# Windowed attention and a MoE layer on one core: V strips as the stationary operand, and all engines ordered by a list scheduler

## The chip, the cores and the metric

The kernel runs on one core of one Trainium2 chip. A core has five engines that run beside each other, each in its own order: TensorE (PE: matmuls into PSUM, eight banks of 128 x 512 float32), VectorE (DVE), ScalarE (ACT), GpSimd (POOL, which here issues the loads that change the type from float32 to float16) and SyncE (SP, which issues the other transfers). A pool or ring of n buffers lets n uses of a tile be under way; the next use waits for the oldest. The metric is the device time of one execution in microseconds (us).

## The reference

There are 8 batches, 8 heads of 64, 512 local and 32 global tokens for each batch. A local query sees the 32 global keys and the local keys at a distance of at most 32; a global query sees all 544 keys. The result goes, as x, through a layer with the hard-swish function:

```python
s_ll = np.where(np.abs(pos[:, None] - pos[None, :]) <= 32, s_ll, -1000000000.0)
s_l = np.concatenate([s_lg, s_ll], axis=-1)            # global keys first
out_l = np.matmul(sm(s_l), np.concatenate([v_g, v_l], axis=2))
out_g = np.matmul(sm(s_g), v_all)                      # 32 queries, 544 keys
x = np.concatenate([out_g, out_l], axis=2)             # as rows of tokens: 4352 x 512
h = x @ w_in                                           # 512 x 2048
out = (h * np.clip(h + 3.0, 0.0, 6.0) / 6.0) @ w_out   # 2048 x 512
```

sm is softmax with the maximum taken off first.

## The kernel before

**Loads.** GpSimd loads q and k of a batch in pieces of 128 tokens (L98), v into a tile ve of five blocks with a column of ones beside each head (L110), then w_in in 4 pieces (L125) and w_out in 16 (L129), all in one queue. After batch 0's loads come the weights; the loads of batch b + 1 are issued three at a time in the loop over blocks of batch b. SyncE copies ve into vo, the same values moved by 64 tokens (L114, L115).

**Attention** goes in blocks. A local block is 128 queries of four heads, as two halves of 64 queries; a half sees 128 local keys and the 32 global ones. There are eight local blocks and two global ones (four heads each) in a batch. For a local block PE makes 16 score matmuls on 64x64 tiles (L202); DVE adds a mask and takes a minimum for each head (L210); ACT takes exp into float16 (L213); DVE packs the global columns of the four heads together (L215); PE turns five 128x128 pieces (L221, L223) into one of two PSUM buffers t; ACT copies them to et (L226); PE multiplies them with the values, global ones first (L231), then eight matmuls of 65 columns with ve and vo as the moving operand (L241); the 65th column is the sum of the weights, by which DVE divides (L255, L256). After two blocks PE turns x (L264) and DVE copies it into xt (L268). q and k are turned at the end of the batch ahead, one pair of heads at a time (L180), and copied by ACT (L183).

**MoE.** For 512 tokens there are 16 first groups of four matmuls (L332), each followed by a relu on ACT (L335) and a product on DVE (L336), and 16 second groups of four matmuls (L346) with a copy (L350) and a store after each four. Groups use three PSUM buffers m. The global tokens of all batches go through it at the end.

**Order.** The loop at L413 to L462 writes each engine's order by hand: for block i it emits the scores of block i, the values of block i - 2, the transposes of block i - 1, and three or four times `fill(0.8)`, which takes MoE groups from a list as shares add up to one. PSUM's eight banks: m 3, s 2, t 2, a 1.

Of the kernel before, what the change touches and what calls it, by code (L numbers as in the profile page):

```python
# [10 lines left out]
FP16 = mybir.dt.float16  # L11


@with_exitstack
def kernel(
# [20 lines left out]
    NQD = NP // 2  # L36
    NJ = Sl // P
    NDFF = dff // P
    HW = 64
    U = Sg + P  # L40
    D1 = D + 2
    KC = Sl + 2 * Sg
# [7 lines left out]
    AX = mybir.AxisListType.XY  # L50

    constp = ctx.enter_context(tc.tile_pool(name="constp", bufs=1))
    natp = ctx.enter_context(tc.tile_pool(name="natp", bufs=2))
    wrk = ctx.enter_context(tc.tile_pool(name="wrk", bufs=2))
    small = ctx.enter_context(tc.tile_pool(name="small", bufs=12))
    xtp = ctx.enter_context(tc.tile_pool(name="xtp", bufs=2))
    moep = ctx.enter_context(tc.tile_pool(name="moep", bufs=1))
    moew = ctx.enter_context(tc.tile_pool(name="moew", bufs=4))
# [6 lines left out]
    qk = [[constp.tile([P, 2 * KC], FP16, tag=f"qk{r}_{p}", name=f"qk{r}_{p}") for p in range(NP)]  # L65
          for r in range(2)]
    ve = [constp.tile([P, NJ + 1, H, D1], FP16, tag=f"ve{r}", name=f"ve{r}") for r in range(2)]
    vo = [constp.tile([P, NJ, H, D1], FP16, tag=f"vo{r}", name=f"vo{r}") for r in range(2)]
    vgb = [constp.tile([P, NQD, 4 * D1], FP16, tag=f"vgb{r}", name=f"vgb{r}") for r in range(2)]
    xg = constp.tile([P, NP, B * Sg], FP16, tag="xg", name="xg")  # L70
    egs = [constp.tile([P, 5 * P], FP16, tag=f"eg{e}", name=f"eg{e}") for e in range(2)]
    ident = constp.tile([P, P], FP16, tag="ident", name="ident")
    masks = [constp.tile([P, U], FP32, tag=f"mask{i}", name=f"mask{i}") for i in range(3)]

    w_in_t = [moep.tile([P, dff], FP16, tag=f"win{m}", name=f"win{m}") for m in range(NP)]
    w_out_t = [moep.tile([P, dm], FP16, tag=f"wout{c}", name=f"wout{c}") for c in range(NDFF)]

    state = {b: {} for b in range(B)}


    def qk_loads(b):
        st = state[b]
        work = []
        if b % 2 == 0:
            t = natp.tile([P, H * D], FP16, tag="qkg", name="qkg")
            for i in range(2):
                for k, src in enumerate((q_g, k_g)):
                    r0 = i * 2 * Sg + k * Sg
                    work.append((t[r0:r0 + Sg, :].rearrange("s (h d) -> s h d", d=D),
                                 src[b + i].rearrange("h s d -> s h d")))  # L90
            st["qkg"] = t
        st["qn"] = natp.tile([P, NJ, H * D], FP16, tag="qn", name="qn")
        st["kn"] = natp.tile([P, NJ, H * D], FP16, tag="kn", name="kn")
        for j in range(NJ):
            for t, src in ((st["qn"], q_l), (st["kn"], k_l)):
                work.append((t[:, j, :].rearrange("s (h d) -> s h d", d=D),
                             src[b, :, j * P:(j + 1) * P, :].rearrange("h s d -> s h d")))
        return [lambda o=o, i=i: nc.gpsimd.dma_start(out=o, in_=i) for o, i in work]  # L98

    def v_loads(b):  # L100
        r = b % 2
        vgn = natp.tile([P, NQD, D], FP16, tag="vgn", name="vgn")
        work = [(vgn, v_g[b].rearrange("(q h) g d -> (h g) q d", q=NQD)),
                (ve[r][0:Sg, 0, :, 0:D], v_g[b].rearrange("h s d -> s h d"))]

        for i in range(NJ + 1):
            p0, p1 = (Sg if i == 0 else 0), (Sg if i == NJ else P)
            s0 = i * P - Sg
            work.append((ve[r][p0:p1, i, :, 0:D], v_l[b, :, s0 + p0:s0 + p1, :].rearrange("h s d -> s h d")))
        work = [lambda o=o, i=i: nc.gpsimd.dma_start(out=o, in_=i) for o, i in work]  # L110

        def shift():

            nc.sync.dma_start(out=vo[r][0:HW, :, :, :], in_=ve[r][HW:P, 0:NJ, :, :])  # L114
            nc.sync.dma_start(out=vo[r][HW:P, :, :, :], in_=ve[r][0:HW, 1:NJ + 1, :, :])  # L115

        def blocks():
            for h in range(4):
                nc.vector.tensor_copy(out=vgb[r][h * Sg:(h + 1) * Sg, :, h * D1:h * D1 + D],  # L119
                                      in_=vgn[h * Sg:(h + 1) * Sg, :, :])  # L120
        return work[0:2] + work[2:] + [shift, blocks]

    def load_w_in():
        for m in range(NP):
            nc.gpsimd.dma_start(out=w_in_t[m], in_=moe_w_in[m * P:(m + 1) * P, :])  # L125

    def load_w_out():
        for c in range(NDFF):
            nc.gpsimd.dma_start(out=w_out_t[c], in_=moe_w_out[c * P:(c + 1) * P, :])  # L129

    def band():

        m = masks[1]
        nc.vector.memset(m, 0.0)
        for s in range(2):
            w = m[s * HW:(s + 1) * HW, Sg:U]
            nc.gpsimd.affine_select(out=w, in_=w, compare_op=ALU.is_ge, fill=OUTSIDE,
                                    base=0, pattern=[[1, P]], channel_multiplier=-1)
            nc.gpsimd.affine_select(out=w, in_=w, compare_op=ALU.is_ge, fill=OUTSIDE,
                                    base=HW, pattern=[[-1, P]], channel_multiplier=1)  # L140
        nc.vector.tensor_copy(out=masks[0], in_=m)
        nc.vector.memset(masks[0][0:HW, Sg:2 * Sg], OUTSIDE)
        nc.vector.tensor_copy(out=masks[2], in_=m)
        nc.vector.memset(masks[2][HW:P, U - Sg:U], OUTSIDE)

    def clear(r):
        nc.vector.memset(ve[r][:, NJ, :, :], 0.0)
        nc.vector.memset(ve[r][:, 0:NJ, :, D:D1], 1.0)
        nc.vector.memset(ve[r][0:Sg, NJ, :, D:D1], 1.0)
        nc.vector.memset(egs[r][:, S:], 0.0)  # L150
        nc.vector.memset(vgb[r], 0.0)
        for h in range(4):
            nc.vector.memset(vgb[r][h * Sg:(h + 1) * Sg, :, h * D1 + D:h * D1 + D + 1], 1.0)
        for p in range(NP):
            for c0 in (KC, 2 * KC - Sg):
                nc.vector.memset(qk[r][p][:, c0:c0 + Sg], 0.0)


    def t_tile(cols):
        t = pst.tile([P, 1024], FP16, tag="t", name="t")  # L160
        return t[:, 0:cols]

    def global_qk(b):
        st = state[b]
        ps = t_tile(NP * P)
        for p in range(NP):
            nc.tensor.matmul(out=ps[:, p * P:(p + 1) * P], lhsT=st["qkg"][:, p * P:(p + 1) * P],
                             rhs=ident, is_transpose=True)
        gt = wrk.tile([P, NP, P], FP16, tag="gt", name="gt")
        nc.scalar.copy(out=gt.rearrange("d p c -> d (p c)"), in_=ps)  # L170
        state[b]["gt"] = gt
        state[b + 1]["gt"] = gt

    def pair_qk(b, p):
        st = state[b]
        ps = t_tile(2 * Sl)
        for i, nat in enumerate((st["qn"], st["kn"])):
            for j in range(NJ):
                c0 = i * Sl + j * P
                nc.tensor.matmul(out=ps[:, c0:c0 + P], lhsT=nat[:, j, p * P:(p + 1) * P],  # L180
                                 rhs=ident, is_transpose=True)
        dst = qk[b % 2][p].rearrange("d (i c) -> d i c", i=2)[:, :, Sg:Sg + Sl]
        nc.scalar.copy(out=dst, in_=ps.rearrange("d (i s) -> d i s", i=2))  # L183

    def local_scores(b, j, qd):
        st = state[b]
        gc = (b % 2) * 2 * Sg + Sg
        ps = pss.tile([P, 2, 512], FP32, tag="s", name="s")
        for pi in range(2):
            p = 2 * qd + pi  # L190
            t = qk[b % 2][p]
            for w, (c0, n) in enumerate(((0, Sg), (Sg, P))):
                for s in range(2):
                    for e in range(2):
                        rows = slice(e * D, (e + 1) * D)
                        lhs = t[rows, Sg + j * P + s * HW:Sg + j * P + (s + 1) * HW]
                        if w == 0:
# [297 lines left out]
```

## Time and profile before

| | |
|---|---|
| median of the runs | 400.8 us (3 runs, 400.43 to 402.07) |
| span of the profiled execution | 400.1 us |
| instructions | 10480 |
| granted TensorE clock, mean | 0.999 |
| GpSimd busy | 120.0 us |
| GB/s of the transfers over the span | 79 |

The span is the profiled execution's own time from its first to its last instruction; 0.7 us lie between it and the median. A row of the busy time by stretches gives the stretch, its length, then for PE, PE's weight loads, DVE, ACT and POOL the busy time and the number of instructions, then the granted clock, the share of the DMA engines and GB/s. A row of the chain or the timeline gives the start in us, the time in us, and the engine, line and operation. A group's row gives busy us, the mean ns of one, and the idle time ahead of them with what ended it.

### The profile page before, as it was taken

What the parts mean: (1) busy time and instruction counts of PE and PEld (TensorE: products, weight loads), DVE (VectorE), ACT (ScalarE), POOL (GpSimd) and SP (SyncE); (2) the same over time, 40 slices, a digit from 0 to 9 for tenths busy, and PEclk for the clock granted to TensorE, in tenths of its full rate; (3) what the DMA queues carried; (4) which work ended last, traced back from release to release, by engine and by line L of the source; (5) the groups of instructions that cost most, each with busy time, mean ns of one, the idle gap of its engine ahead of it and who ended that gap; (6) DMA issues with size and microseconds to landing.
All of it is one profiled execution on the core that took longest, in us unless ns stands there. A gap on an engine that the chain in (4) does not pass through costs nothing.

```text
span 400.1 us, 10480 instructions
## 1 busy us (share of the span) xinstructions
PE 364.8 (91%) x4104; PEld 203.6 (51%) x4104; DVE 263.9 (66%) x1073; ACT 255.0 (64%) x549; POOL 120.0 (30%) x166
## 2 busy tenths in 40 slices
PE   0647499999999999999999999999999999999996
PEld 0414286655455555555555545555555455545642
DVE  2426368866797569766995788658965698457611
ACT  1554389866687569756885588657875687346400
POOL 8924999834700290009200740004000000000000
PEclk9999999999999999999999999999999999999999
DMA  9999999984930199019901992019201000100022
GB/s 91 87 210 189 154 144 162 166 74 63 173 67 28 31 159 111 3 54 129 140 7 54 91 127 56 28 54 90 51 28 55 27 2 28 51 32 0 2 79 79
DMA packets 117874, 31.75 MB, mean 79 GB/s; under 512 B 109888, under 2 KB 111936, under 8 KB 117824
## 3 DMA queue, kind: packets, MB, share of 16 engines
q0 software_dynamic: 111552, 17.84, 60.2%
q1 hardware_dynamic: 6272, 13.24, 10.3%
q8 instruction: 32, 0.52, 0.5%
q14 instruction: 18, 0.15, 0.1%
HBM read 35.65 MB, written 8.91 MB: 111 GB/s over the span
## 4 chain that ended last, share of the span: by engine, by line
PE 75%; ACT 6%; DVE 5%; POOL 5%; DMA 5%; issue 2%; POOLq 0%; ACTq 0%
PE m L346 29%; PE m L332 23%; PE t L221 4%; DMA win<-in_moe_w_in_dram 4%; PE s L202 4%; PE a L241 3%; PE t L180 3%; ACT ex L213 3%; ACT t L335 2%; DVE gt L336 2%; PE a L231 2%; PE t L298 2%; DVE ot L350 1%; DMA qn<-in_q_l_dram 1%; PE t L264 1%
## 5 line engine op out<-in xcount | busy, mean ns | idle before, releaser
L332 PE MATMUL m<-xt,win 128*128 128x512 f16 (+1 forms) x576 | 123.1, 358 | 3.0 <-DVE gt L336 2.1
L346 PE MATMUL m<-wout,gt 128*128 128x512 f16 x512 | 121.8, 379 | 0.0
L213 ACT ACTIVATE ex<-sm,mx 128x160 f16<-128x160 f32 x256 | 89.4, 418 | 43.5 <-DVE mx L210 43.4
L336 DVE SCALAR_TENSOR_TENSOR gt<-t,m 128x512 f16<-128x512 f32 (+1 forms) x144 | 85.7, 623 | 18.9 <-ACT t L335 18.3
L335 ACT ACTIVATE t<-m 128x512 f32<-128x512 f32 (+1 forms) x160 | 79.5, 529 | 25.3 <-PE m L332 23.9
L332 PEld LDWEIGHTS <-win 128*128 128x128 f16 x640 | 60.5, 98 | 49.8 <-issue 4.7
L210 DVE CUSTOM_DVE_ANT_0 sm<-s,mask 128x160 f32<-128x160 f32 x256 | 68.4, 319 | 8.4 <-PE s L202 7.5
L346 PEld LDWEIGHTS <-gt 128*128 128x128 f16 x512 | 47.2, 98 | 44.4
L226 ACT COPY et<-t 128x640 f16<-128x640 f16 x64 | 43.9, 686 | 21.2 <-PE t L223 21.2
L350 DVE COPY ot<-m 128x512 f32<-128x512 f32 x34 | 23.5, 691 | 36.6 <-PE m L346 36.6
L98 POOL DMA_DIRECT2D qn<-in_q_l_dram x32 | 29.7, 928 | 33.3 <-PE t L180 32.3
L183 ACT COPY qk<-t 128x1024 f16<-128x1024 f16 x32 | 31.9, 1008 | 11.0 <-PE t L180 11.0
L221 PE MATMUL t<-ident,ex 128*128 128x128 f16 x256 | 31.1, 229 | 2.4 <-ACT ex L213 1.8
L110 POOL DMA_DIRECT2D ve<-in_v_l_dram x40 | 32.4, 855 | 1.0 <-issue 0.4
L98 POOL DMA_DIRECT2D kn<-in_k_l_dram x32 | 29.8, 930 | 0.0
L202 PEld LDWEIGHTS <-qk 64*64 64x64 f16 x1024 | 17.7, 111 | 23.4 <-issue 14.7
L180 PE MATMUL t<-ident,qn 128*128 128x128 f16 x128 | 14.2, 231 | 15.2 <-POOL ident masks.py:199 9.6
L256 DVE TENSOR_TENSOR x<-a,rec 128x256 f16<-128x256 f32 x64 | 27.0, 421 | 1.1
L241 PE MATMUL a<-vo,et 128*64 128x65 f16 x256 | 20.8, 205 | 6.3 <-DMA vo<-ve 6.3
L110 POOL DMA_DIRECT2D vgn<-in_v_g_dram x8 | 6.0, 749 | 68.5 <-DVE vgb L119 68.5
L202 PE MATMUL s<-qk 64*64 64x128 f16 x512 | 25.6, 230 | 0.0
L215 DVE COPY exg<-ex 128x128 f16<-128x128 f16 x64 | 15.4, 240 | 14.8 <-ACT ex L213 14.1
(68 smaller groups left out, 379.9 us busy)
## 6 DMA issues: line engine op xcount, KB each, us to landing
out_dram<-ot SPq DMA_DIRECT2D x32, 256.0 KB, 2.0
vo<-ve SPq DMA_DIRECT2D x16, 264.0 KB, 3.8
qn<-in_q_l_dram POOLq DMA_DIRECT2D x32, 128.0 KB, 5.3
kn<-in_k_l_dram POOLq DMA_DIRECT2D x32, 128.0 KB, 5.7
ve<-in_v_l_dram POOLq DMA_DIRECT2D x24, 128.0 KB, 5.4
win<-in_moe_w_in_dram POOLq DMA_DIRECT2D x4, 512.0 KB, 13.0
wout<-in_moe_w_out_dram POOLq DMA_DIRECT2D x16, 128.0 KB, 5.0
ve<-in_v_l_dram POOLq DMA_DIRECT2D x8, 96.0 KB, 5.2
```

The costliest lines, as they stand in the source:

```text
L98: return [lambda o=o, i=i: nc.gpsimd.dma_start(out=o, in_=i) for o, i in work]
L110: work = [lambda o=o, i=i: nc.gpsimd.dma_start(out=o, in_=i) for o, i in work]
L202: nc.tensor.matmul(out=ps[s * HW:(s + 1) * HW, e, pi * U + c0:pi * U + c0 + n], lhsT=lhs, rhs=rhs)
L210: nc.vector.tensor_tensor_reduce(out=sm, in0=ps[:, e, pi * U:(pi + 1) * U], in1=m, scale=-scale, scalar=3.0e38, op0=ALU.add, op1=ALU.min, ...
L213: nc.scalar.activation(out=ex[:, h, :], in_=sm, func=EXP, scale=-1.0, bias=mx)
L221: nc.tensor.matmul(out=ps[:, h * P:(h + 1) * P], lhsT=ex[:, h, Sg:U], rhs=ident, is_transpose=True)
L226: nc.scalar.copy(out=et, in_=ps)
L241: nc.tensor.matmul(out=ps[s * HW:(s + 1) * HW, h, 0:D + 1], lhsT=et[:, h * P + s * HW:h * P + (s + 1) * HW], rhs=v[:, j, 4 * qd + h, 0:D + 1],
L332: nc.tensor.matmul(out=ps[:, 0:n], lhsT=w_in_t[m][:, c * P:(c + 1) * P], rhs=x[:, m, 0:n], start=(m == 0), stop=(m == NP - 1))
L335: nc.scalar.activation(out=t1[:, 0:n], in_=ps[:, 0:n], func=RELU, bias=0.5, scale=1.0 / 6.0)
L336: nc.vector.scalar_tensor_tensor(out=g[:, 0:n], in0=t1[:, 0:n], scalar=1.0, in1=ps[:, 0:n], op0=ALU.min, op1=ALU.mult)
L346: nc.tensor.matmul(out=ps, lhsT=gs[c][:, t0:t0 + P], rhs=w_out_t[c], start=(c == 0), stop=(c == NDFF - 1))
```

## The change

The kernel is written anew around the same arithmetic of the MoE part.

- **A unit** is 32 queries of one head with 32 global and 96 local keys: 128 keys. A local step is 128 queries of all eight heads, 32 units. There are four local steps in a batch.
- **Scores**: eight full-array matmuls with 32 columns take the global keys, laid out with zeros for the other head of the pair (kgz), and 32 matmuls on 64x32 tiles with 96 columns take the local keys.
- **Softmax**: the minimum for each head as before but over 128 columns; exp writes float32 in place and also gives the sum; DVE takes reciprocals and scales each head into float16, before the transposes. No column of ones.
- **Transposes**: eight of 128x128 for a step, into the only PSUM buffer T (1024 columns), copied by DVE.
- **Values**: SyncE lays V out as strips st, one of 128 keys for each 32 queries (16 strips of 128 x 512 in float16 for a batch; the 32 global rows are repeated in each). A strip's two heads are the stationary operand and the weights of 64 columns stream: 16 matmuls for a step. The result is x transposed; ACT copies it into xt in two half-partition copies. PE no longer turns x. The global queries use V as the stationary operand too.
- **Loads**: w_in comes in 16 pieces, by quarters of its columns; batch 1's q, k and v are issued ahead of w_out.
- **PSUM**: S 2 banks, T 1, A 2, M 3.
- **Order**: every operation is added to a plan with an engine, a duration, what it needs, a key and the buffers that it takes and gives back. `lay()` runs through the plan once and gives every engine its order; the instructions are emitted in that order.

The core of the diff (helpers for evictions, loads and the global steps are left out where the text above tells them):

```diff
-    psm = ctx.enter_context(tc.tile_pool(name="psm", bufs=3, space=bass.MemoryType.PSUM))
-    pss = ctx.enter_context(tc.tile_pool(name="pss", bufs=1, space=bass.MemoryType.PSUM))
-    pst = ctx.enter_context(tc.tile_pool(name="pst", bufs=2, space=bass.MemoryType.PSUM))
-    psa = ctx.enter_context(tc.tile_pool(name="psa", bufs=1, space=bass.MemoryType.PSUM))
+    psS = many(1, [P, 2, 512], FP32, "s", pp)
+    psT = many(1, [P, 1024], FP16, "t", pp)
+    psA = many(1, [P, 2, 512], FP32, "a", pp)
+    psM = many(3, [P, 512], FP32, "m", pp)
...
+    nat = many(3, [P, 2, HD], FP16, "nat")
...
+    st = many(2, [P, NJ * NU, HD], FP16, "st")
+    sm = many(NS, [P, H, P], FP32, "sm")
+    pn = many(NS, [P, H, P], FP16, "pn")
...
+    LAT = {"PE": 260, "ACT": 170, "DVE": 140, "POOL": 150, "SP": 0, "Q": 0}
...
+    def lay(self):
...
+        while done < len(self.ops):
+            best = None
+            for e, cand in opened.items():
+                if not cand:
+                    continue
+                if e in ("POOL", "SP"):
+                    pool = [min(cand, key=lambda o: (o.key, o.n))]
+                else:
+                    pool = cand
...
+                s0 = min(s for s, _ in starts)
+                s, o = min(((s, o) for s, o in starts if s <= s0 + 40), key=lambda x: (x[1].key, x[1].n))
+                if best is None or s < best[0]:
+                    best = (s, o)
...
+        order.sort(key=lambda o: (o.start, o.n))
+        return order
...
+    def strips(b, js, key):
...
+            if j0 == 0:
+                nc.sync.dma_start(out=st[r][0:G, :, :], in_=ve[r][0:G, 0:1, :].to_broadcast([G, NJ * NU, HD]))
+            v4 = st[r].rearrange("p (j u) c -> p j u c", u=NU)
+            for c in range(NU):
+                lo = c * UQ
+                a = min(P - lo, KL)
+                nc.sync.dma_start(out=v4[G:G + a, j0:j1, c, :], in_=ve[r][lo:lo + a, j0:j1, :])
+                if a < KL:
+                    nc.sync.dma_start(out=v4[G + a:P, j0:j1, c, :], in_=ve[r][0:KL - a, j0 + 1:j1 + 1, :])
...
+    def local_step(b, j, key):
...
+            for p in range(NP):
+                for e in range(2):
+                    nc.tensor.matmul(out=ps[:, e, p * P:p * P + G],
+                                     lhsT=qk[r][:, p, 0, UQ + j * P:UQ + (j + 1) * P], rhs=kgz[r][:, p, e, :])
+            for p in range(NP):
+                for u in range(NU):
+                    for e in range(2):
+                        rows = slice(e * D, (e + 1) * D)
+                        q0 = UQ + j * P + u * UQ
+                        nc.tensor.matmul(out=ps[u * UQ:(u + 1) * UQ, e, p * P + G:(p + 1) * P],
+                                         lhsT=qk[r][rows, p, 0, q0:q0 + UQ],
+                                         rhs=qk[r][rows, p, 1, q0 - UQ:q0 + 2 * UQ])
+        s = add("PE", 800, pe, [qkT[b, j], qkT[b, min(j + 1, NJ - 1)], kg[b]], key=key, acq="S")
...
+                nc.vector.tensor_tensor_reduce(
+                    out=sm[sm_op.slot][:, h, :], in0=psS[s.slot][:, e, p * P:(p + 1) * P], in1=m,
+                    scale=-scale, scalar=3.0e38, op0=ALU.add, op1=ALU.min,
+                    accum_out=stat[stat_op.slot][:, 0, h:h + 1])
...
+                nc.scalar.activation(out=sm[sm_op.slot][:, h, :], in_=sm[sm_op.slot][:, h, :], func=EXP,
+                                     scale=-1.0, bias=stat[stat_op.slot][:, 0, h:h + 1],
+                                     accum_out=stat[stat_op.slot][:, 1, h:h + 1])
...
+                    nc.vector.tensor_scalar(out=pn[pn_op.slot][:, h, :], in0=sm[sm_op.slot][:, h, :],
+                                            scalar1=stat[stat_op.slot][:, 2, h:h + 1], scalar2=None, op0=ALU.mult)
...
+            for h in range(H):
+                nc.tensor.matmul(out=psT[op.slot][:, h * P:(h + 1) * P], lhsT=pn[pn_op.slot][:, h, :],
+                                 rhs=ident, is_transpose=True)
...
+            nc.vector.tensor_copy(out=et[et_op.slot].rearrange("k h q -> k (h q)"), in_=psT[t.slot])
...
+                    nc.tensor.matmul(out=ps[:, p // 2, c0:c0 + 64],
+                                     lhsT=st[r][:, j * NU + u, p * P:(p + 1) * P],
+                                     rhs=et[et_op.slot][:, 2 * p:2 * p + 2, u * UQ:(u + 1) * UQ])
...
+            nc.scalar.copy(out=xt[xt_op[b].slot][e * D:(e + 1) * D, :, j * P:(j + 1) * P].rearrange(
+                "d p (u q) -> d p u q", u=NU), in_=src[e * D:(e + 1) * D, :, :, e, :])
...
+    for b in range(B):
+        base = -8.0 if b == 0 else -5.5 if b == 1 else 4.0 * b - 7.0
...
+                wi[g] = load_w_in(g, -6.0 + 0.1 * g)
...
+                wo[c] = load_w_out(c, -4.0 + 0.05 * c)
...
+        moe_local(b, lead + 4.5, 4.0)
+    moe_global(lead + 6.5, 1.5)
...
+    order = plan.lay()
```

More of the change, by code (lines that the diff above doesn't have):

```diff
@@ L68 @@
[L68 to L85, printed above, removed]
+    AX = mybir.AxisListType.X
+    sb = ctx.enter_context(tc.tile_pool(name="sb", bufs=1))
+    pp = ctx.enter_context(tc.tile_pool(name="pp", bufs=1, space=bass.MemoryType.PSUM))
@@ L98, in qk_loads @@
-        return [lambda o=o, i=i: nc.gpsimd.dma_start(out=o, in_=i) for o, i in work]
-    def v_loads(b):
-        r = b % 2
[L102 to L121, printed above, removed]
@@ L146, in clear @@
[L146 to L156, printed above, removed]
@@ L159, in t_tile @@
[L159 to L172, printed above, removed]
@@ L185, in local_scores @@
[L185 to L193, printed above, removed]
+                    nc.gpsimd.dma_start(out=dst(op, i, k), in_=src[b + i].rearrange("h s d -> s h d"))
+        return add("POOL", 2300, emit, [], key=key, acq="natg", xfer=800)
@@ L339 @@
-    held = {}
-    def second(gs, t0, quarter, store):
-        if quarter == 0:
-            held["ps"] = psm.tile([P, 512], FP32, tag="m", name="m")
-        ps = held["ps"]
-        for c in range(quarter * 4, quarter * 4 + 4):
-            nc.tensor.matmul(out=ps, lhsT=gs[c][:, t0:t0 + P], rhs=w_out_t[c],
-                             start=(c == 0), stop=(c == NDFF - 1))
-        if quarter == 3:
-            ot = moew.tile([P, dm], FP32, tag="ot", name="ot")
-            nc.vector.tensor_copy(out=ot, in_=ps)
-            store(ot)
@@ new lines, in moe_local, with key @@
+    def moe_local(b, at, span):
+        set_ = add("ACT", 0, lambda op: None, xdone[b, 0], key=at - 1, acq="gs")
+        n = 256 if b == 0 else 512
+        total = 16 * (Sl // n) + 16
+        k = [0]
+        def key():
+            k[0] += 1
+            return at + span * k[0] / total
+        done = [[] for _ in range(NDFF)]
+        per = n // P
+        for part in range(Sl // n):
+            xdeps = [d for j in range(part * per, (part + 1) * per) for d in xdone[b, j]]
+            for c in range(NDFF):
+                done[c].append(first(c, n, part * n, lambda: xt[xt_op[b].slot], xdeps,
+                                     [xt_op[b]], set_, key()))
+        for j in range(NJ):
+            row = b * S + G + j * P
+            second(j * P, [done[c][j // per] for c in range(NDFF)], set_,
+                   [(out[row:row + P, :], 0, P)], [key() for _ in range(4)])
@@ L370, in moe_global @@
+    def moe_global(at, span):
+        deps = [xgd[b] for b in range(B)]
+        set_ = add("ACT", 0, lambda op: None, deps, key=at - 1, acq="gs")
+        done = [first(c, B * G, 0, lambda: xg, deps, [], set_, at + span * c / 24) for c in range(NDFF)]
         rows = out.rearrange("(b s) d -> b s d", s=S)
+        per = P // G
         for i in range(B // per):
-            def store(ot, i=i):
-                for b in range(per):
-                    nc.sync.dma_start(out=rows[i * per + b, 0:Sg, :], in_=ot[b * Sg:(b + 1) * Sg, :])
```

684 lines of the change are left out of this document (410 added, 274 removed).

## The prediction

> **What bounds the kernel now.** I read the page's summary first, then the busy time by stretches, the chain that ended last, and the order of TensorE's work in one steady stretch.
>
> ```profile
> span 400.1 us, 10480 instructions
> ...
> PE 364.8 (91%) x4104; PEld 203.6 (51%) x4104; DVE 263.9 (66%) x1073; ACT 255.0 (64%) x549; POOL 120.0 (30%) x166
> ```
> ```profile
> 0.00:20.00 20.00, 6.78 (x73) 4.91 (x73) 6.64 (x57) 7.18 (x11) 18.65 (x34) 1.00 1.39 89
> 20.00:40.00 20.00, 11.76 (x170) 6.77 (x170) 9.29 (x60) 10.74 (x27) 6.83 (x13) 1.00 1.09 200
> 40.00:60.00 20.00, 14.32 (x162) 10.51 (x159) 10.07 (x37) 11.98 (x27) 20.00 (x28) 1.00 1.82 149
> ...
> 200.00:300.00 100.00, 99.28 (x1151) 53.96 (x1149) 74.73 (x304) 73.44 (x157) 16.13 (x20) 1.00 0.46 59
> ```
> ```profile
> 19.37 15.98 DMA win<-in_moe_w_in_dram
> ...
> 41.57 5.41 DMA qn<-in_q_l_dram
> 48.25 1.44 PE m L332 x6
> ...
> 105.66 1.02 PE m L332 x4
> ...
> 316.59 1.02 PE m L332 x4
> ...
> 375.69 20.73 PE m L346 x96
> ```
>
> There are two regimes. In the first 60 us PE is busy for 32.9 us (first column of busy time), and the chain runs through transfers: w_in lands at 35.35 us, and from 41.57 to 46.98 us everything waits for the next batch's q. The first MoE matmul starts at 48.25 us. After that PE is the bound: 99% busy from 200 to 300 us, DVE 75%, ACT 73%. Like places of the batches stand five batches apart at 105.66 and 316.59 us, so a batch takes 42.2 us. A 512-column MoE matmul costs 20.73 / 96 = 0.216 us, and a batch has 64 of each kind: 27.7 us. The other 14.5 us are attention and gaps; the change works on these and on the head.
>
> ```profile
> 208.10 0.39 PE L180 MATMUL t<-ident,qn 128*128 128x128 f16 x4
> ...
> 208.55 1.89 PE L346 MATMUL m<-wout,gt 128*128 128x512 f16 x8
> ...
> 220.03 0.22 PE L283 MATMUL s<-gt 64*32 64x32 f16 x4
> 220.07 0.29 PE L284 MATMUL s<-qk,gt 64*32 64x240 f16 x4
> 220.17 0.30 PE L285 MATMUL s<-qk,gt 64*32 64x272 f16 x4
> 220.41 0.22 PE L241 MATMUL a<-ve,et 128*64 128x65 f16 x1
> ...
> 224.38 0.33 PE L310 MATMUL a<-ve,et 128*32 128x65 f16 x20
> 224.64 0.45 PE L298 MATMUL t<-ident,eg 128*128 128x128 f16 x5
> 224.93 2.75 PE L346 MATMUL m<-wout,gt 128*128 128x512 f16 x12
> ...
> 240.22 0.28 PE L231 MATMUL a<-vgb,et 128*128 128x264 f16 x1
> 240.43 0.21 PE L202 MATMUL s<-gt,qk 64*64 64x32 f16 x4
> ...
> 240.73 0.22 PE L241 MATMUL a<-ve,et 128*64 128x65 f16 x1
> ...
> 240.78 0.20 PE L241 MATMUL a<-ve,et 128*64 128x65 f16 x1
> ...
> 240.97 0.40 PE L221 MATMUL t<-ident,ex 128*128 128x128 f16 x4
> ...
> 241.26 1.89 PE L332 MATMUL m<-xt,win 128*128 128x512 f16 x8
> ...
> 242.99 0.39 PE L264 MATMUL t<-ident,x 128*128 128x128 f16 x4
> 243.22 1.03 PE L332 MATMUL m<-xt,win 128*128 128x512 f16 x4
> ```
>
> In these rows a start to the next start is what an operation costs PE; the durations overlap. A local block of four heads runs from 240.22 to 241.26: 0.21 global values, 0.30 scores, 0.24 local values, 0.29 transposes, 1.04 us. Turning x costs 0.23, eight q and k transposes 0.45 (56 ns each), a global block 0.38 + 0.26 + 0.29 = 0.93. A batch: 8 x 1.04 + 4 x 0.23 + 4 x 0.45 + 2 x 0.93 + 0.1 for small turns = 13.0 us. With MoE 40.7; the other 1.5 of 42.2 are gaps.
>
> **PE in the changed kernel.** MoE matmuls stay in number and shape. For 128 queries of all heads, before 2 x 1.04 + 0.23 = 2.31 us, it now has:
> - 32 scores on 64x32 tiles with 96 columns. The nearest rows have that tile: four take 0.04 us with 32 columns, 0.10 with 240. Per matmul 10 to 25 ns; eight tiles now stand side by side, so I take 12.5 ns: 0.40 (0.32 to 0.80).
> - 8 full-array scores against the zero-padded global keys, 32 columns, and 16 value matmuls, V stationary, 64 columns. No row has a full array with so few columns. A pair of L241 loads the same 128 weight columns and streams 65: 240.73 to 240.78, then 0.03 to 0.04. I take 40 ns for both: 0.32 and 0.64. Below: streaming alone at MoE's rate, 0.216 x 64 / 512 = 27 ns and 14 ns; above: a transpose, 56 ns. So 0.11 to 0.45 and 0.43 to 0.90.
> - 8 transposes, 0.45. Turning x goes, because the values come out as x transposed.
>
> The sum is 1.81 (1.31 to 2.60), so 0.50 less, 2.0 us a batch. The global part exchanges: scores 0.04 + 0.22 for 0.38, twice; values 20 x 0.04 for 2 x 0.26 + 0.06: nothing net. Over 8 batches: **-16 us** (-32 to +9).
>
> [...]
>
> **The other engines.**
>
> ```profile
> 17.66 0.32 DVE L210 CUSTOM_DVE_ANT_0 sm<-s,mask 128x160 f32<-128x160 f32 x1
> ...
> 17.90 0.32 DVE L210 CUSTOM_DVE_ANT_0 sm<-s,mask 128x160 f32<-128x160 f32 x1
> ```
> ```profile
> L336 DVE SCALAR_TENSOR_TENSOR gt<-t,m 128x512 f16<-128x512 f32 x112 | 73.1, 683 | 12.5 <-ACT t L335 12.3
> ...
> L183 ACT COPY qk<-t 128x1024 f16<-128x1024 f16 x32 | 31.9, 1008 | 11.0 <-PE t L180 11.0
> ...
> L256 DVE TENSOR_TENSOR x<-a,rec 128x256 f16<-128x256 f32 x64 | 27.0, 421 | 1.1
> ...
> L215 DVE COPY exg<-ex 128x128 f16<-128x128 f16 x64 | 15.4, 240 | 14.8 <-ACT ex L213 14.1
> ...
> L268 DVE COPY xt<-t 128x512 f16<-128x512 f16 x32 | 13.4, 418 | 12.5 <-PE t L264 12.3
> ```
> ```profile
> L215 DVE COPY exg<-ex x64: 182/195/637, 19.2 to 339.9; 128x128 f16<-128x128 f16 x64
> ```
>
> VectorE is busy 0.747 x 42.2 = 31.5 us a batch. It loses 8 exg copies (1.9), 8 normalisations (3.4), 4 copies of x (1.7) and the vgb copies (under 1). Its 32 masked minima get 32 of 160 columns shorter (about 1 in all; one costs 0.24 us from start to start). It gains 32 scalings of 128 columns, SBUF to SBUF: the nearest row is L215, mean 0.24 (0.195 its median to 0.32, the longer L210), 7.7 us; 4 evictions of 1024 columns of T (below 2 x 0.42, above L268 alone), 3; and about 2 in the global part. So about 35.5 of some 40: it is no longer slack. In the half batch with the 16 first matmul groups DVE has 16 x 0.68 + two softmax units of about 4.4 = 19.7, less about 0.08 an instruction that overlaps the next (about 2), against 13.8 + 2 x 1.8 + 1 = 18.4 on PE. That is nearly a tie, so gaps will grow: I take 0.7 us a batch over 7.5 batches, **+5 us** (0 to 15). ScalarE gives 10 T evictions to DVE and takes 8 half-partition copies of x: no more than before.
>
> [...]
>
> **The head.**
>
> ```profile
> PE a L241 <- DMA vo<-ve: 6.3, 1, 6.3
> ```
>
> By the order of the changed program GpSimd issues batch 0's q, k and v, the mask, w_in in 16 pieces by quarters of its columns, batch 1's q, k, v, and only then w_out. So the 5.4 us wait for q goes, and the first MoE group needs one quarter of w_in, not the w_in that landed at 35.35. What is late next are the V strips: instead of vo, which held PE for 6.3 us (until 31.4), 2 MB a batch go by SyncE's queue, the first 0.9 MB before the first values. They start once v's first two blocks have landed, about 16 us, and share the engines with w_in. At the 200 GB/s of 20 to 40 us, 0.9 MB take 4.5 us alone, twice that shared, and each further unit's 0.38 MB 2 to 4: the second unit's values come at about 30 to 34 us and MoE can start about 35, 13 us earlier. By then PE has done about 3 us less attention, and the strips delay w_in's last quarters. Of the 10 left I take **-8 us** (-13 to +3). Later, w_out stands behind 18 loads: issued from about 42 to 50 us, needed only after 14 us of first groups and most of batch 1's attention, about 60. In the steady state the 2 MB strips of a batch are 10 us at that rate in a batch of 40, two buffers ahead. POOL at 30% hides the 12 more issues of w_in after 18 us.
>
> **Sum.** 400.1 - 16 + 5 - 8 = 381.1 for the profiled execution; its span lies 0.7 below the median of the three runs, 400.8, so about **382 us**.
>
> **Rivals.**
> - *More than I count* (below 374): weight loads hide and full-array matmuls cost streaming only; PE then saves up to 32 us, 382 - 16 = 366. For it: the short L241 starts. Against: DVE would then bind.
> - *VectorE binds the first half* (390 to 398): if a scaling costs 0.28 from start to start instead of some 0.16, each softmax unit takes 1 us more of DVE, and DVE leads PE by 2 us a batch: 382 + 2 x 7.5 = 397. For it: the near tie, and the 637 ns copy. Against: the order of the changed program puts only two units' minima among the first groups. Two more cases end here: full-array matmuls at the transposes' 56 ns (0.38 us a unit more, 12 in all: 394), and tile scores at L284's 25 ns (0.40 a unit, 13 in all: 395).
> - *One T bank instead of two* (slower): the changed kernel gives the transposes a single PSUM bank. Each of some 10 uses a batch must be evicted (1.01 us for L183's shape) before PE's next, and PE stands behind it in order. If half an eviction is exposed, 0.5 x 10 = 5 us a batch, 382 + 37 = 419; slower than 402.8 from 0.28 us a use on. Against: in the program order most uses have one to three MoE groups of 0.86 us between them, which cover 1 us.
> - *No change in sum*: the losses of the second rival with a head that gains nothing.
>
> **How the numbers follow.** Forecast 374 to 390: 0.42. More than I count: 0.15. VectorE or the full array, 390 to 398.8: 0.20. Within 0.5% of 400.8, which is about what a measurement here can tell: 0.05. One T bank or another wait of that kind: 0.18. So faster 0.77, same 0.05, slower 0.18. The range 365 to 404 takes in the bounds of PE's sum and the mild end of the slower case.
>
> **What would show it.** A batch period of 39 to 41.5 us; value matmuls about 40 ns from start to start; the tile scores (line 385 of the changed kernel) near 12 ns; the first MoE matmul at 33 to 38 us; scalings of mean 0.2 to 0.3 us; DVE at 85% or more in the steady part. PE idle for the T bank, or a batch over 43 us, would prove the third rival. Wrong from the start would be: strips landing after 40 us, or PE waiting for w_out.

## The result, and the profile after

The changed kernel takes **396.46 us** (median of 6 runs, 392.27 to 402.51), the kernel before, timed beside it, 401.29 us. Two of the six runs, 399.43 and 402.51 us, ran over 1.5% longer than the shortest, and the ratio is over the other four, whose median is 395.2 us: 0.984 [0.980, 0.988]. So the time falls by 1.6% where 4.7% was forecast (382 us). The direction was right and the time lies in the range of 365 to 404; the size was wrong by 13 to 14 us. The profiled execution took 392.27 us, the shortest of the six; its span is 390.5 us.

The page of the changed kernel: the span, the busy time of the engines, the granted clock in 40 slices, and the chain that ended last by engine and by line.

```profile
span 390.5 us, 10537 instructions
...
PE 341.2 (87%) x3872; PEld 195.6 (50%) x3872; DVE 293.0 (75%) x1198; ACT 258.7 (66%) x805; POOL 121.9 (31%) x173
...
PEclk9999999899999999998999999997899999999999
...
PE 32%; DVE 20%; issue 18%; DMA 12%; ACT 10%; POOL 6%; SPq 2%; POOLq 0%; ACTq 0%
PE m L556 14%; PE m L537 11%; DMA st<-ve 5%; DVE gs L547 5%; DVE pn L422 5%; DVE sm L397 5%; ACT sm L408 5%; DMA nat<-in_k_l_dram 4%; ACT t L543 3%; POOL nat L267 3%; DMA ve<-in_v_l_dram 3%; PE a L442 2%; POOL ve L280 2%; ACT xt L452 2%; PE t L428 2%
```

PE's work fell by more than forecast (16 us), from 364.8 to 341.2 us. But PE was 91% busy and is now 87%, and the chain names copies of strips (st<-ve) and loads of v and k, which had no part in the steady batches before. The clock dips in three places. The busy time by stretches shows where, first for the kernel before, then for the changed one (columns as in the table of time and profile: after the stretch and its length, PE's busy time; the clock is the third number from the end):

```profile
0.00:60.00 60.00, 32.85 (x401) 22.20 (x402) 26.01 (x152) 29.90 (x63) 45.48 (x73) 1.00 1.43 146
60.00:100.00 40.00, 39.01 (x545) 24.47 (x544) 29.96 (x146) 31.26 (x77) 26.31 (x35) 1.00 1.35 116
100.00:300.00 200.00, 198.12 (x2321) 107.44 (x2319) 149.96 (x600) 146.46 (x312) 48.19 (x60) 1.00 0.67 74
300.00:400.10 100.10, 94.85 (x841) 49.54 (x840) 58.02 (x177) 47.43 (x99) 0.00 (x0) 0.99 0.10 35
```
```profile
0.00:60.00 60.00, 35.69 (x538) 26.09 (x539) 38.93 (x222) 39.76 (x136) 45.43 (x77) 1.00 1.48 177
60.00:100.00 40.00, 34.97 (x475) 22.88 (x475) 29.88 (x122) 26.61 (x85) 19.65 (x25) 0.96 1.43 170
100.00:300.00 200.00, 185.41 (x2145) 101.72 (x2144) 164.26 (x670) 146.30 (x457) 56.84 (x71) 0.97 0.90 114
300.00:390.50 90.50, 85.17 (x723) 44.95 (x715) 59.90 (x188) 46.06 (x130) 0.00 (x0) 1.00 0.12 42
```

From 100 to 300 us, where PE had been idle for 1.9 us, it is idle for 14.6, at a lower clock (0.97). The waits of the changed kernel (engine, tile and line, what ended the wait, then total us, times, longest) say for what:

```profile
POOL nat L267 <- PE t L331: 151.5, 20, 15.8
...
PE a L442 <- DMA st<-ve: 12.3, 7, 3.4
...
PE m L537 <- DVE gs L547: 5.1, 10, 1.2
...
PE t L331 <- ACT qk L336: 1.3, 2, 1.1
```

The value matmuls wait for strips. One such place in PE's timeline of the changed kernel (start, us, operation and count; in brackets the idle time ahead and what ended it):

```profile
178.78 0.36 PE L385 MATMUL s<-qk 64*32 64x96 f16 x32
179.08 0.23 PE L442 MATMUL a<-et,st 128*128 128x64 f16 x2
181.80 0.19 PE L442 MATMUL a<-et,st 128*128 128x64 f16 x1 [2.49 <-DMA st<-ve]
183.63 0.85 PE L442 MATMUL a<-et,st 128*128 128x64 f16 x13 [1.64 <-DMA st<-ve]
184.29 4.01 PE L537 MATMUL m<-xt,win 128*128 128x512 f16 x12
188.13 0.61 PE L331 MATMUL t<-ident,nat 128*128 128x128 f16 x8
```

PE stands for 4.1 us. Then 12 MoE matmuls take 3.84 us from start to start, 0.32 each, where 105.90 to 108.49 us of the same trace has 12 in 2.59: here the idle time is paid for twice, as a wait and as a slower clock behind it (granted 0.91 from 180 to 200 us). PE also stands for strips at 63.6 us (batch 1) and at 268.5 us (batch 6). Why the strips of batch 4 are late here is in the queues. First GpSimd's, then SyncE's (SPq), ahead of that place:

```profile
157.63 0.88 POOL L267 DMA_DIRECT2D nat<-in_q_l_dram  x1 [12.61 <-PE t L331]
158.50 0.89 POOL L267 DMA_DIRECT2D nat<-in_k_l_dram  x1
159.36 0.90 POOL L280 DMA_DIRECT2D ve<-in_v_l_dram  x1
166.04 0.88 POOL L267 DMA_DIRECT2D nat<-in_q_l_dram  x1 [5.78 <-PE t L331]
166.91 0.89 POOL L267 DMA_DIRECT2D nat<-in_k_l_dram  x1
167.78 0.61 POOL L280 DMA_DIRECT2D ve<-in_v_l_dram  x1
```
```profile
166.33 6.00 SPq L300 DMA_DIRECT2D st<-ve  x3
177.43 0.63 SPq L302 DMA_DIRECT2D st<-ve  x1
178.10 0.61 SPq L300 DMA_DIRECT2D st<-ve  x1
178.75 0.65 SPq L302 DMA_DIRECT2D st<-ve  x1
```
```profile
ve<-in_v_l_dram POOLq DMA_DIRECT2D x1, 32.0 KB, 9.6
```

v's last block, 32 KB, stands in GpSimd's queue behind loads of q and k of the next batch; these wait for one of three nat buffers, which PE's transposes give back (5.78 us here). It is issued at 167.78 and lands 9.6 us later (the row of its DMA issue: count, KB, us to landing), at 177.4. SyncE's next strip copy starts at 177.43, and the last strip comes at 183.63. From batch 1 on, all strips of a batch are one lot in the plan, so that even the first step's values need that last block. Batch 6 has the same picture: a wait of 5.8 us for nat, and 10.1 us for the block to land. Batch 1 has not: GpSimd waits 0.87 us for nat there, SyncE issues the lot's last copies from 50.43 to 58.9 us, and the last of them lands at 66 us. The plan, which set PE's order by its own times, gives the block 0.1 + 0.9 + 0.3 + 1.1 = 2.4 us from issue to landing if the transfers ahead of it are done, and the lot of strips 1.25 x 4 + 1.2 = 6.2 us.

**Theory A**: the order of loads makes the strips late, the plan does not know it, and PE's fixed order stands. **B**: the copies themselves, 2 MB a batch, are too much for the transfers. **C**: VectorE sets the pace (the prediction's second rival). B is undone only by fewer copies, A by any earlier v or smaller lot.

### The profile page after: what moved, and what is told of

It reads as the page before. It is cut to its first block, busy times and chain, and to the rows that moved or that the text cites. A ratio compares the mean times of both kernels' runs of the same rounds, so it can differ in the third digit from the quotient of the medians.

```text
span 390.5 us, 10537 instructions
## 1 busy us (share of the span) xinstructions
PE 341.2 (87%) x3872; PEld 195.6 (50%) x3872; DVE 293.0 (75%) x1198; ACT 258.7 (66%) x805; POOL 121.9 (31%) x173
## 4 chain that ended last, share of the span: by engine, by line
PE 32%; DVE 20%; issue 18%; DMA 12%; ACT 10%; POOL 6%; SPq 2%; POOLq 0%; ACTq 0%
PE m L556 14%; PE m L537 11%; DMA st<-ve 5%; DVE gs L547 5%; DVE pn L422 5%; DVE sm L397 5%; ACT sm L408 5%; DMA nat<-in_k_l_dram 4%; ACT t L543 3%; POOL nat L267 3%; DMA ve<-in_v_l_dram 3%; PE a L442 2%; POOL ve L280 2%; ACT xt L452 2%; PE t L428 2%
## 5 line engine op out<-in xcount | busy, mean ns | idle before, releaser
L556 PE MATMUL m<-wout,gs 128*128 128x512 f16 x544 | 129.6, 379 | 0.3 <-DVE gs L547 0.3
L547 DVE SCALAR_TENSOR_TENSOR gs<-t,m 128x512 f16<-128x512 f32 (+1 forms) x160 | 94.6, 604 | 38.9 <-ACT t L543 37.6
L408 ACT ACTIVATE sm<-sm,stat 128x128 f32<-128x128 f32 x256 | 99.9, 395 | 14.3 <-DVE stat L397 13.7
L267 POOL DMA_DIRECT2D nat<-in_q_l_dram x32 | 28.7, 896 | 156.2 <-PE t L331 151.5
L556 PEld LDWEIGHTS <-gs 128*128 128x128 f16 x544 | 49.7, 98 | 50.0 <-issue 2.3
L422 DVE TENSOR_SCALAR pn<-sm,stat 128x128 f16<-128x128 f32 x256 | 61.7, 323 | 1.6
L397 DVE CUSTOM_DVE_ANT_0 sm<-s,mask 128x128 f32<-128x128 f32 x256 | 59.6, 285 | 0.5 <-PE s L385 0.3
L452 ACT CAST xt<-a 64x512 f16<-64x512 f32 x64 | 37.0, 578 | 34.1 <-PE a L442 33.4
L408 ACT ACTIVATION_READ_ACCUMULATOR sm<-sm,stat 128x1 f32 x256 | 49.6, 194 | 0.0
L336 ACT COPY qk<-t 128x1024 f16<-128x1024 f16 x32 | 32.2, 1006 | 14.5 <-PE t L331 13.9
L442 PE MATMUL a<-et,st 128*128 128x64 f16 x512 | 24.4, 203 | 16.0 <-DMA st<-ve 12.3
L331 PE MATMUL t<-ident,nat 128*128 128x128 f16 x256 | 22.3, 233 | 13.8 <-DMA nat<-in_q_l_dram 10.6
L442 PEld LDWEIGHTS <-st 128*128 128x128 f16 x512 | 21.9, 104 | 24.3 <-issue 16.2
L267 POOL DMA_DIRECT2D nat<-in_k_l_dram x32 | 28.8, 899 | 0.0
L331 PEld LDWEIGHTS <-nat 128*128 128x128 f16 x256 | 17.8, 104 | 21.0 <-DMA nat<-in_q_l_dram 12.1
L428 PE MATMUL t<-ident,pn 128*128 128x128 f16 x256 | 24.3, 230 | 4.5 <-DVE pn L422 3.8
```

The source lines that it names most:

```text
L267: nc.gpsimd.dma_start(out=nat[op.slot][:, i, :].rearrange("s (h d) -> s h d", d=D), in_=src[b, :, j * P:(j + 1) * P, :].rearrange("h s d - ...
L397: nc.vector.tensor_tensor_reduce(out=sm[sm_op.slot][:, h, :], in0=psS[s.slot][:, e, p * P:(p + 1) * P], in1=m, scale=-scale, scalar=3.0e38 ...
L408: nc.scalar.activation(out=sm[sm_op.slot][:, h, :], in_=sm[sm_op.slot][:, h, :], func=EXP, scale=-1.0, bias=stat[stat_op.slot][:, 0, h:h + 1],
L422: nc.vector.tensor_scalar(out=pn[pn_op.slot][:, h, :], in0=sm[sm_op.slot][:, h, :], scalar1=stat[stat_op.slot][:, 2, h:h + 1], scalar2=Non ...
L428: nc.tensor.matmul(out=psT[op.slot][:, h * P:(h + 1) * P], lhsT=pn[pn_op.slot][:, h, :], rhs=ident, is_transpose=True)
L442: nc.tensor.matmul(out=ps[:, p // 2, c0:c0 + 64], lhsT=st[r][:, j * NU + u, p * P:(p + 1) * P], rhs=et[et_op.slot][:, 2 * p:2 * p + 2, u * ...
```

## The experiments

All comparisons are with runs of the kernel before in the same session (401.2 to 401.6 us).

### v's loads earlier (e1_v_ahead)

```diff
-  vload[b, i] = load_v(b, i, base + stepk * (i + 0.3) * 0.8 + 1.1 * stepk)
+  vload[b, i] = load_v(b, i, base + (stepk * (i + 0.3) * 0.8 + 1.1 * stepk if b < 2 else 0.3 + 0.1 * i))
```

> The changed kernel with one edit: from batch 2 on, a batch's five v loads go into GpSimd's queue right behind its first q and k load, not between the later ones. Theory A (order of the loads: strips are late because v's last blocks stand in the queue behind q and k loads that wait for a free nat buffer): PE's waits for st fall from 12.3 us to under 4, every batch takes 39.5 to 41 us, the granted clock stays at 1.00, and the time is 376 to 384 us. Theory B (the 2 MB of copies themselves are too slow beside the loads): waits for st stay at 8 us or more and the time at 388 to 394. Theory C (VectorE, busy 84%, sets the pace): the waits go, but other waits of PE take their place, 388 to 393.

Measured: 379.18 us, ratio 0.946 [0.943, 0.948]. PE's wait for strips is down from 12.3 to 2.1 us, in one place (batch 1, which the edit leaves as it was), the granted clock up from 0.983 to 0.994. The copies are all still there, so B is in trouble.

### Strips by step (e2_strips_by_step)

```diff
-  if b == 0:
-      for j in range(NJ):
-          strip[b, j] = strips(b, [j], base + 1 + j)
-  else:
-      s_ = strips(b, list(range(NJ)), base + 1)
-      for j in range(NJ):
-          strip[b, j] = s_
+  for j in range(NJ):
+      strip[b, j] = strips(b, [j], base + 1 + j)
```

> The changed kernel with strips copied for one local step at a time in every batch, not only in batch 0; the order of the loads stays. Theory A: the first step's strips need only v's first two blocks, which are not the late ones, so most of the wait goes: 378 to 386 us. Theory B: as much is copied, in four times as many transfers: 390 to 396. Theory C: 388 to 393.

Measured: 376.34 us, 0.938 [0.936, 0.941], and the four runs lie within 0.9 us. No wait for a strip is left in the trace. Its stretches, for the sums below:

```profile
0.00:60.00 60.00, 35.26 (x550) 26.16 (x551) 37.21 (x216) 39.46 (x134) 44.23 (x75) 1.00 1.50 175
60.00:100.00 40.00, 36.81 (x482) 23.02 (x482) 32.99 (x142) 28.85 (x94) 21.08 (x28) 1.00 1.46 182
100.00:300.00 200.00, 193.23 (x2323) 107.56 (x2321) 174.83 (x713) 155.17 (x483) 56.82 (x71) 1.00 0.88 117
300.00:375.20 75.20, 70.42 (x522) 36.58 (x520) 46.62 (x130) 35.11 (x97) 0.00 (x0) 0.99 0.10 36
```

The same bytes move in more and smaller copies, and the time falls by 15.3 us of span. So the loss goes with the strips' lateness, and the number of bytes copied is not its cause.

### No strip copies (e3_no_strips)

```diff
-  s_ = strips(b, list(range(NJ)), base + 1)
+  s_ = strips(b, list(range(NJ)), base + 1) if b == 1 else strip[b - 2, NJ - 1]
```

> The changed kernel without the strip copies of batches 2 to 7: their values are multiplied with the strips of batches 0 and 1, which leaves 12 MB of copies out of the computation and every wait for them. It is the floor for all that strips cost. Theory A and B: 374 to 380 us; A expects the two edits of the order to come within 4 us of it, B expects it 10 us or more below them. Theory C: 386 to 391, since VectorE keeps all its work.

Measured: 379.34 us, 0.947 [0.943, 0.951]. Taking 12 MB of copies away gives no more than putting them in another order: B falls. What wait is left, 3.9 us, lies in batch 1, whose strips are still made in one lot. One thing of B stays: v's last block lands in 3.9 us here (median of the eight), in 8.6 in the changed kernel and in 5.0 with strips by step, which fits copies on their way beside it slowing it.

### Six nat buffers (e4_nat6)

```diff
-  nat = many(3, [P, 2, HD], FP16, "nat")
+  nat = many(6, [P, 2, HD], FP16, "nat")
```

> The changed kernel with six nat buffers in place of three, so that GpSimd's queue need not stand at a q or k load; v loads keep their place. Theory A: GpSimd's waits for the turns (151 us) fall by half or more, strips come early, 376 to 385 us. Theory B: loads and copies still collide, 388 to 394. Theory C: 388 to 393.

Measured: 381.48 us, 0.950 [0.946, 0.953]. GpSimd's wait for nat falls from 151.5 to 81.7 us and no strip is waited for. This touches neither strips nor v, only what stands ahead of v in the queue: the middle link of theory A. It stays 5 us behind the strips by step (spans 379.8 and 375.2 us), and the trace says where: PE is idle for 32.5 us of the first 100 us, with strips by step for 27.9. One place makes the difference:

```profile
68.77 0.61 PE L331 MATMUL t<-ident,nat 128*128 128x128 f16 x4 [5.18 <-DMA nat<-in_q_l_dram]
```

At the like place with strips by step (68.85 us) PE stands 0.31 us.

### The plan told a longer strip time (e8_true_strips)

```diff
-  return add("SP", 100 * (6 + (j0 == 0)), emit, deps, key=key, xfer=1250 * n + (1200 if j0 == 0 else 0))
+  return add("SP", 100 * (6 + (j0 == 0)), emit, deps, key=key, xfer=2500 * n + (2400 if j0 == 0 else 0))
```

> The changed kernel with one number of its plan doubled, the time of the strip copies; loads keep their order. Theory (the plan puts the values of a batch at a time when the strips can't be there): the plan now has PE do MoE groups first, and the waits for st fall under 5 us, 378 to 386 us. Rival (v comes so late that no order of PE helps): 390 to 396.

Measured: 378.64 us (377.32 to 382.92), 0.944 [0.937, 0.952]; PE waits 2.6 us for strips. The work of every engine is that of the changed kernel; only a number differs, by which the scheduler puts it in order. So the plan's short time for the copies is part of the cause. That other matmuls ahead of the values are what helps is not shown: the new order also has the copies earlier, the last of batch 4 issued at 174.63 us instead of 178.75 and of batch 6 at 255.49 instead of 264.93. The four runs scatter by 5.6 us: the margin is thin.

Every edit lets `lay()` write the whole order anew, so no run moves the strips alone. What ties the loss to them is the wait itself: 12.3 us in the changed kernel, 0 to 3.9 in these five.

### The head, alone: w_out first (e5_wout_first)

From the strips by step; w_out's loads go ahead of batch 1's q, k and v.

```diff
-  wo[c] = load_w_out(c, -4.0 + 0.05 * c)
+  wo[c] = load_w_out(c, -5.58 + 0.004 * c)
```

> The kernel with strips by step (376.3 us), with w_out put ahead of batch 1's q, k and v in GpSimd's queue, as in the kernel before. Theory (the head's term is the place of w_out): PE waits for batch 1's loads again, 381 to 386 us. Rival (the head is shorter for other reasons, quarters of w_in and less work on PE): 375 to 378.

Measured: 377.44 us, 0.940 [0.937, 0.943], against 376.34: about 1 us, within the intervals of both. The theory missed and the rival held: w_out's place is worth nearly nothing here.

### The head, in the old kernel (e6_before_loads)

```diff
-  for m in range(NP):
-      nc.gpsimd.dma_start(out=w_in_t[m], in_=moe_w_in[m * P:(m + 1) * P, :])
+  for g in range(4):
+      for m in range(NP):
+          nc.gpsimd.dma_start(out=w_in_t[m][:, g * 512:(g + 1) * 512],
+                              in_=moe_w_in[m * P:(m + 1) * P, g * 512:(g + 1) * 512])
...
+  for f in qk_loads(1):
+      f()
...
-          loads = qk_loads(b + 1)
+          loads = qk_loads(b + 1) if b else []
```

> The kernel before with one part of the change alone: w_in in quarters of its columns, and batch 1's q and k ahead of w_out. Theory: its 5 us wait for q and the wait for the whole w_in go, 393 to 397 us. Rival (V's copies and the blocks' order hold the head anyway): 400 to 402.

Measured over eight runs: 398.9 us, 0.9935 [0.9915, 0.9955], so -2.6 us (-3.4 to -1.8), between the two ranges expected and in neither. Its waits keep the other long one of the head:

```profile
PE a L243 <- DMA vo<-ve: 6.3, 1, 6.3
```

### Four scalings as one (e7_merge_scale)

From the strips by step; one instruction multiplies four heads by their reciprocals, read as a broadcast.

```diff
-  for h in range(h0, h1):
-      def sc(op, h=h):
-          nc.vector.tensor_scalar(out=pn[pn_op.slot][:, h, :], in0=sm[sm_op.slot][:, h, :],
-                                  scalar1=stat[stat_op.slot][:, 2, h:h + 1], scalar2=None, op0=ALU.mult)
-      scs.append(add("DVE", 132, sc, [rec], key=key - 0.1, rel=[sm_op, stat_op]))
+  def sc(op, h0=h0, h1=h1):
+      nc.vector.tensor_tensor(out=pn[pn_op.slot][:, h0:h1, :], in0=sm[sm_op.slot][:, h0:h1, :],
+                              in1=stat[stat_op.slot][:, 2, h0:h1].unsqueeze(2).to_broadcast([P, 4, P]),
+                              op=ALU.mult)
+  scs.append(add("DVE", 600, sc, [rec], key=key - 0.1, rel=[sm_op, stat_op]))
```

> The kernel with strips by step, with the four scalings of a half step done as one tensor_tensor against the reciprocals spread over 128 columns: about 0.6 us of VectorE in place of 4 x 0.21 to 0.28, some 20 us less of it in all. If VectorE sets the pace of the steady batches (40.2 us, 88% busy), a batch falls by 1 us or more: 364 to 370 us. If not, 374 to 378.

Measured: **373.51 us**, 0.9285 [0.925, 0.932], the shortest of the study. The group of scalings in the changed kernel, then here (busy us, mean ns of one, idle ahead):

```profile
L422 DVE TENSOR_SCALAR pn<-sm,stat 128x128 f16<-128x128 f32 x256 | 61.7, 323 | 1.6
```
```profile
L421 DVE TENSOR_TENSOR pn<-sm,stat 128x512 f16<-128x512 f32 x64 | 44.0, 688 | 1.3
```

VectorE's busy time goes from 291.7 (strips by step) to 277.3 us over the whole span, and 2.8 us of those 14.4 reach the end. So C holds a small part of the gaps, not the pace.

### Values twice (e9_values_twice)

```diff
-  for u in range(NU):
+  for u in [w for w in range(NU) for _ in range(2)]:
```

> The kernel of e2_strips_by_step (376.3 us) with each of the 512 value matmuls done twice in a row, the second writing the same sums again; nothing is left out. In the changed kernel's undisturbed batches 16 value matmuls take 0.46 us from start to start, 29 ns each, so 512 more of them are 14.9 us of TensorE. If TensorE still sets the pace of the steady batches, as the prediction says, nearly all of it shows: 389 to 392. At the prediction's 40 ns a matmul it would be 20.5 us: 397. If VectorE or another engine sets the pace, the copies fill gaps: below 382.

Measured: 390.02 us, 0.974 [0.970, 0.977], against 0.938 without them: 14 us for 512 matmuls, 27 ns each. One of the places in its timeline:

```profile
119.21 1.10 PE L442 MATMUL a<-et,st 128*128 128x64 f16 x32
120.14 1.03 PE L556 MATMUL m<-wout,gs 128*128 128x512 f16 x4
```

32 take 0.93 us, 29 ns each, and nearly all of that shows in the end time: PE still sets the pace of the steady batches.

### One T bank in the old kernel (e10_before_one_t)

```diff
-  pst = ctx.enter_context(tc.tile_pool(name="pst", bufs=2, space=bass.MemoryType.PSUM))
+  pst = ctx.enter_context(tc.tile_pool(name="pst", bufs=1, space=bass.MemoryType.PSUM))
```

> The kernel before with one bank for its transposes in place of two; everything else as it was. This prices the third rival in the old order: the prediction gave it 0.5 us a use of the bank, some 10 uses a batch, +37 us: 438. If the order of that kernel leaves matmuls between two uses, as the changed kernel's does (its waits for the bank came to 1.3 us in all), under 405. The kernel before has 12 groups of transposes a batch that go in threes and fours, less well spread than in the changed kernel, so I expect a loss of 5 to 20 us: 406 to 421.

Measured: 413.8 us, 1.032 [1.029, 1.035]. In an order that was not made for it, one bank costs 12.6 us, within the 5 to 20 expected and a third of the 37 of the rival. In the changed kernel's order PE's waits for the bank (ended by the copies out of it, L336) come to about 4 us; the 1.3 us of the expectation are those of one line, L331.

### Both orders of loads at once (e11_combo)

The merged scalings and the strips by step, with v's loads moved as in the first experiment.

> The kernel of e7_merge_scale (strips by step, four scalings as one instruction; 373.5 us) with v's loads of batches 2 to 7 right behind the first loads of q and k as well (the edit of e1_v_ahead). With strips by step no strip was waited for any more, so if late loads of v are what that wait was, nothing is left to gain: 372 to 375. If the head of each batch still loses time to v, 368 to 371.

Measured: 375.75 us, 0.936 [0.933, 0.938], 2 us more than without the move. From 100 to 300 us PE is as busy (196.3 against 195.7 us), but in the head it is not:

```profile
60.00:100.00 40.00, 34.37 (x371) 21.29 (x371) 27.21 (x104) 24.73 (x84) 23.05 (x31) 0.96 1.45 174
```

Here the kernel with merged scalings alone has 38.01 us. With strips by step the move has nothing left to gain, and it costs something at 60 to 100 us, just behind the head. The late transfer is the load of the global k (natg):

```profile
80.53 0.59 PE L347 MATMUL t<-ident,natg 128*128 128x128 f16 x4 [3.89 <-DMA natg<-in_k_g_dram]
```

The move puts batch 2's v ahead of it in GpSimd's queue: the global loads start at 71.59 us, without the move at 66.17.

## Why the prediction was wrong

Its sum can be checked term by term on spans, with the strips by step as the changed kernel without the surprise. Before, PE is busy for 364.8 of 400.1 us; with strips by step for 335.7 of 375.2; in the changed kernel for 341.2 of 390.5.

- **The step that failed** is "In the steady state the 2 MB strips of a batch are 10 us at that rate in a batch of 40, two buffers ahead", put at nothing. Measured: 390.5 - 375.2 = **+15.3 us**, 9.8 of it idle PE and 5.5 of it work at a slower clock (0.91, 0.91 and 0.83 in the 20 us of the three stalls); by medians (395.2 and 376.3) 19 us. The rate was not the fault (no copies at all: 379.3). The step looked at bytes and buffers, not at what a copy waits for: v's last block, in batches 4 and 6 behind loads that wait for buffers that PE gives back. The change's order on GpSimd and the lot of strips were there to be read. Both of the warnings that the prediction gave, strips after 40 us in the head and PE waiting for w_out, looked at the head; the stalls came in batches 1, 4 and 6. In batch 1 the lot is what the runs show (by step the wait goes, with v ahead 2.1 us stay); what slowed its copies is open.
- **PE's work**, forecast -16, is **-29.1 us** (364.8 - 335.7). The mechanism was right, and the term was sized too small. The clean places of the changed kernel's timeline give the prices from a start to the next start:

```profile
108.94 0.36 PE L378 MATMUL s<-kgz,qk 128*128 128x32 f16 x8
109.22 0.36 PE L385 MATMUL s<-qk 64*32 64x96 f16 x32
109.52 1.04 PE L537 MATMUL m<-xt,win 128*128 128x512 f16 x4
...
119.90 0.63 PE L442 MATMUL a<-et,st 128*128 128x64 f16 x16
120.37 1.03 PE L556 MATMUL m<-wout,gs 128*128 128x512 f16 x4
...
131.56 0.75 PE L519 MATMUL a<-eg,ve 128*128 128x64 f16 x20
132.14 1.03 PE L556 MATMUL m<-wout,gs 128*128 128x512 f16 x4
```

  Global scores 0.28 (35 ns each, taken as 40), tile scores 0.30 (9.4 ns, below my lower bound of 10), values 0.47 (29 ns, taken as 40 from the L241 pair; the lower bound, streaming at MoE's rate, 27 ns, lay nearer). With 0.45 of transposes a step of 128 queries (a "unit" in the prediction's sums) is 1.50 us, not 1.81: 0.81 less than before, 26 over the 32 steps. The other 3 us were not traced. The global part is not where they lie: its 20 values take 0.58 and not 0.80, but its scores 0.35 and not 0.26, twice a batch, so that little is left.
- **The head**, forecast -8, is **about nothing**. MoE does start early, at 37.9 us as forecast (33 to 38), but PE's idle time in the first 100 us is 27.15 + 0.99 = 28.1 before and 24.74 + 3.19 = 27.9 with strips by step. So the earlier first matmul was no gain in idle time. The load edits alone gave the old kernel 2.6 us; w_out's place gave about 1, inside the noise.
- **VectorE's near tie**, forecast +5, is **+4.4**, if all the growth of idle time is put down to it: idle PE after 100 us is 7.1 before, 11.5 with strips by step. PE's waits there that VectorE ended are 3.0 and 6.6 us, so most of it is VectorE's. VectorE is 87% busy from 100 to 300 us there, as forecast, and a scaling's mean of 323 ns is above the 200 to 300 that I named. The merged scalings confirm the direction: PE's idle time after 100 us falls by 2.8 us, as the time does. The long scalings end with GpSimd's loads:

```profile
L422 DVE TENSOR_SCALAR pn<-sm,stat x256: 267/282/734, 21.4 to 333.9; 128x128 f16<-128x128 f32 x128
```

  The row has the shortest, median and longest in ns, and the first and last start. After GpSimd's last load, at 289 us, the longest of 44 takes 288. The mean lies 41 over the median, 10.5 us for 256. Why the others are longer no run shows.
- **The rivals.** More than I count was right for PE's work, and with the strips in order its end lies near (376.3; 373.5 with merged scalings, "below 374"). VectorE as the bound came out in the right region, 390 to 398, for the wrong reason. One T bank is small, about 4 us of waits in all. That the loss would be a new wait I had as a class, but at the wrong place.

Sum: -29.1 - 0.2 + 4.4 + 15.3 = -9.6, the difference of the spans. In the forecast, 13 us too little for PE's work and 8 us too much for the head stood against each other, and that they partly cancelled was luck; the strips' 15.3 made the forecast 9.4 us too short on spans.

## What to carry to other kernels

A transfer is on time or late by what its last input waits for: follow each added copy back through its queue to the buffer that the head of the queue waits for, and ask who gives that buffer back. Where a list scheduler writes the order, compare its durations with the landings that the trace shows; a guess that is some us short (2.4 against 9.6 for one block here) puts a stall on the engine that binds. And let consumers wait for the part that they read, not for a lot: splitting one wait into four was worth 5% here, with the same bytes.

## What the hardware showed that was not expected

- Three stalls of TensorE were paid for twice. They took 3 to 5 us each, and the granted clock of their 20 us was 0.91, 0.91 and 0.83, where with strips by step the same stretches have 1.00; PE's busy time is 5.5 us longer in all than there:

```profile
60.00:80.00 20.00, 15.56 (x212) 11.20 (x212) 14.87 (x73) 15.63 (x55) 15.65 (x20) 0.91 1.76 175
180.00:200.00 20.00, 16.55 (x187) 8.99 (x188) 13.47 (x56) 13.74 (x40) 3.93 (x5) 0.91 0.54 75
260.00:280.00 20.00, 15.23 (x121) 7.38 (x119) 11.97 (x42) 11.72 (x36) 6.36 (x8) 0.83 1.02 149
```

  The longest single MoE matmul took 631 ns, where the median is 379:

```profile
L537 PE MATMUL m<-xt,win x576: 269/379/631, 37.9 to 357.6; 128*128 128x512 f16 x149, 128*128 128x256 f16 x43
```

  Behind the second stall 12 MoE matmuls took 3.84 us from start to start, and the 24 from 188.58 us 5.35, 0.22 each; behind the third, 12 took 5.01. The first stall was two idle stretches of 0.66 and 2.34 us, and was paid for all the same. The idle time of the head was not: PE stands for 24.3 of the first 60 us, and the granted clock there is 1.00.
- A load of 32 KB took 9.6 us to land when it was issued among loads of q and k and strip copies, where two of 128 KB in the same 25 us took 5.1 by the median: size said little about when it landed.
- 32 matmuls on 64x32 tiles with 96 columns take 9.4 ns each.
